# Attention and a mixture of experts on one Trainium2 core: the scale of w2 from sums of squares on ScalarE, the first block's scores in alternating row halves, the first block under the planner

## The chip, the cores and the metric

The kernel runs on one core of one Trainium2 chip, as one program. The metric is the device time of a run in microseconds (us). The engines are TensorE (PE for its matmuls, PEld for its weight loads), VectorE (DVE), ScalarE (ACT), GpSimd (POOL) and SyncE (SP), which here only issues DMAs. Each engine works through its own queue in order; semaphores tie the queues together.

## The reference

Attention comes first, over 4 batches of 8 heads, 768 positions and 64 columns. Each query sees the keys within 16 positions of it and one summary per block of 32 keys (the maximum of the keys, the mean of the values):

```python
k_sum = k.reshape(B, H, nb, block, D).max(axis=3)
v_sum = v.reshape(B, H, nb, block, D).mean(axis=3)
scores_l = scale * q @ k.T          # masked to |i - j| < 16
scores_s = scale * q @ k_sum.T + log(32)
a = softmax(concat(scores_l, scores_s)); out = a @ concat(v, v_sum)
```

Its output, as 3072 tokens of 512 columns, goes through four experts of 1024 hidden columns, and every token takes all four:

```python
p = domain_probs / (domain_probs.sum(-1) + 1e-9)
for e in range(4): out += p[:, e:e+1] * (maximum(x @ w1[e], 0) @ w2[e])
```

## The kernel before, in words

**Tiles.** Attention goes in 64 pieces: 96 queries of 4 heads each (`n` counts them, 16 to a batch). The experts take tokens in eight blocks of 384 (`tb`). Eight pieces make a block. The first block (pieces of queries 0 to 383 of batch 0) has code of its own, `first_tokens`, since no expert can start without it. Blocks 0 and 1 then go through the experts alone for experts 0 and 1 (stages `[0]` and `[1]` of `plan`, full-precision products `ph` and `po`); after that blocks go in pairs (`PAIRS`; pair 0 is blocks 0 and 1 with experts 2 and 3, pairs 1 to 3 have all four). A pair's first product is done in seven half-size products instead of eight (`pha`, `phb`, `phc`, `phd`), from sums and differences of tokens (`x_operands`, tiles `x_` and `x_t`) and weights (`w1_operands`, tiles `w1g`), each split in two 16-bit parts.

**A piece of the first block.** `scores` makes the products of 96 queries with 128 keys and 24 summaries, head by head, in two halves (two heads each, one PSUM tile `psc` each, from a pool of two); `maxima` on VectorE adds the mask and takes each row's maximum, `exps` on ScalarE the exponentials, `turn` transposes them on TensorE (`pT`), `gather` multiplies with the values (`pav`), `divide` normalises on VectorE, `x_turn` transposes again, `x_part` writes the two parts `xh` and `xl` of the tokens. A head's 64 columns lie in 64 of the 128 rows of the array: heads 0 and 2 of a piece in the upper half, 1 and 3 in the lower.

**Scales.** The 16-bit parts need a scale per expert. For each of w1 and w2 of an expert, `scan` loads the weights once more in eight tiles of 128x512 (`ws`, two buffers), and `largest` takes each row's largest magnitude on VectorE into `wmax`: 64 reductions for four experts. After an expert's last tile `scales_of_weights` takes the maximum (`wm`), and `scales` turns it by TensorE, spreads it and inverts it in a chain of small VectorE steps (`dg`, `big`, `scale`, `one`). Only then can that expert's `w1g` and `w2s` be made.

**What sets the order.** All instructions are recorded as steps and given out by a planner, `order_of`. It simulates the engines with costs per step (`Step.PE`, `Step.ACT` and so on, `SPARE` above them), takes at each moment the ready step that is due first, does this several times forward and backward (`ROUNDS`) and keeps its shortest plan. Steps before `in_order` keep the order in which they were written: in the kernel before, the whole first block does on every engine, with an order by hand (`KEYS`, `T0`, `STEPS`), and on SP besides. In which order attention's steps are recorded among the experts' is set by `ENDS`: the piece that attention has reached at the end of each stage. `XFREE` gives odd pieces below that number a second set of buffers, and `early` says how long before a stage's end the next pair's `x_operands` are recorded. Nearly every instruction is issued by one helper line, L373 in the profile of the kernel before.

## Time and profile before

| | us |
|---|---|
| median of 3 runs | 1080.83 (1080.18 to 1082.72) |
| the profiled execution, its own time | 1079.39 |
| its span, first to last instruction | 1077.5 |
| TensorE busy | 1051.8 (98%) |
| VectorE, ScalarE, GpSimd busy | 866.0, 730.2, 607.2 |
| mean granted TensorE clock | 0.995 |

The profiled execution is 1.89 us longer than its span, and 1.44 us under the median. In rows of a timeline the first column is the start in us from the span's start, the second the duration; a bracket at the end is idle time of that engine just before, and what ended it. In rows by stretch, each engine has its busy time in that stretch and its number of instructions, then come the granted clock, the busy share of the DMA engines and GB/s. In rows of groups, the two numbers behind the bar are busy us and mean ns of one. In rows by tile, the three durations are the least, the median and the largest in ns, and the two numbers after them the first and the last start.

### The profile page before, as it was taken

The page shows a single profiled execution, that of the slowest core. Times are in us where ns is not written, and L with a number is a line of the kernel's source. Part 1 is how long each engine was busy: PE and PEld are TensorE (multiplying, and loading weights), DVE is VectorE, ACT ScalarE, POOL GpSimd, SP SyncE. Part 2 cuts the span into 40 slices and gives each one's busy share as a digit, 9 for nine tenths or more (in the row PEclk, how much of TensorE's full clock was granted, in tenths as well). Part 3 has the DMA queues.
Part 4 walks back from the last instruction along what each step waited for, and adds up shares of the span by engine and source line. Part 5 has one row for each costly group of instructions (what it writes and reads, how often), then busy time and mean ns, then how long its engine had stood idle before and what let it go on. Part 6 is the DMA issues. An engine that isn't in the chain of part 4 may idle for free.

```text
span 1077.5 us, 22082 instructions
## 1 busy us (share of the span) xinstructions
PE 1051.8 (98%) x7497; PEld 707.7 (66%) x7497; DVE 866.0 (80%) x2102; ACT 730.2 (68%) x1992; POOL 607.2 (56%) x716
## 2 busy tenths in 40 slices
PE   9988999899999999999999999999999999999998
PEld 7977888654554555555555568686775567686867
DVE  6898889988877867988988897998767775969473
ACT  5776688887864744976977796988545763748170
POOL 2599588877743211852856887896532352717050
PEclk9999999989999999999999999999999999999999
DMA  8789887987888889789676664657422440424001
GB/s 287 212 202 244 227 220 198 274 270 198 240 245 253 253 232 254 220 268 263 207 231 170 167 176 126 176 163 217 116 83 89 135 149 16 162 66 151 1 15 59
DMA packets 172897, 194.95 MB, mean 181 GB/s; under 512 B 80368, under 2 KB 117232, under 8 KB 172784
## 3 DMA queue, kind: packets, MB, share of 16 engines
q1 hardware_dynamic: 172784, 193.55, 62.3%
q8 instruction: 58, 0.95, 0.4%
q14 instruction: 55, 0.45, 0.1%
HBM read 141.33 MB, written 35.65 MB: 164 GB/s over the span
## 4 chain that ended last, share of the span: by engine, by line
PE 66%; DVE 5%; POOL 2%; ACT 2%; DMA 1%; issue 1%; SPq 0%; DVEq 0%; POOLq 0%; ACTq 0%
PE po L373 16%; PE phb L373 13%; PE pha L373 8%; PE pob L373 7%; PE poa L373 5%; PE phd L373 4%; PE phc L373 4%; PE poc L373 3%; PE pod L373 2%; PE psc L373 2%; PE px L373 1%; POOL w2g L373 1%; DVE wr L373 1%; DMA wr<-in_w2L 1%; ACT ms L373 0%
## 5 line engine op out<-in xcount | busy, mean ns | idle before, releaser
L373 PEld LDWEIGHTS <-w1g 128*128 128x128 f16 x2352 | 229.2, 98 | 174.2 <-issue 13.0
L373 PEld LDWEIGHTS <-h 128*128 128x128 f16 x1764 | 171.0, 98 | 115.9 <-issue 0.5
L373 PE MATMUL po<-w2s,h 128*128 128x512 f16 x1008 | 239.6, 379 | 0.0
L373 PE MATMUL phb<-x_t,w1g 128*128 128x384 f16 x1008 | 195.3, 327 | 4.6 <-DVE phc L373 1.9
L373 POOL TENSOR_TENSOR w2g<-wr,w2g 128x512 f16<-128x512 f32 (+1 forms) x80 | 90.1, 1133 | 114.3 <-ACT w2g L373 112.1
L373 PE MATMUL pha<-x,w1g 128*128 128x384 f16 x672 | 133.3, 329 | 2.9 <-DVE nb L373 2.9
L373 ACT ACTIVATE ms<-ms,nb 96x152 f32<-96x152 f32 x256 | 104.0, 414 | 15.5 <-DVE nb L373 15.2
L373 PEld LDWEIGHTS <-hs 128*128 128x128 f16 x1008 | 98.0, 98 | 12.7 <-issue 0.4
L373 POOL TENSOR_TENSOR v<-qv,v 128x256 f16<-128x256 f32 (+1 forms) x56 | 45.7, 816 | 104.6 <-ACT v L373 89.7
L373 DVE CUSTOM_DVE_ANT_0 ms<-psc,c_sb 96x152 f32<-96x152 f32 x256 | 69.1, 305 | 31.3 <-PE psc L373 30.5
L373 POOL TENSOR_TENSOR h<-r,h 128x384 f16<-128x384 f32 x56 | 57.1, 1025 | 54.1 <-ACT h L373 51.5
L373 ACT CAST w2g<-wr 128x512 f16<-128x512 f32 (+1 forms) x112 | 61.6, 562 | 32.2 <-DVE wr L373 18.7
L373 POOL TENSOR_TENSOR w<-wr,w 128x512 fp32r<-128x512 f32 x48 | 65.3, 1368 | 26.2 <-ACT w L373 20.3
L373 DVE TENSOR_TENSOR aw<-ms,aw 96x512 f16<-96x512 f32 (+1 forms) x104 | 69.7, 686 | 6.3 <-ACT aw L373 6.3
L373 PE MATMUL ph<-xh,w 128*128 128x384 f32 x256 | 69.4, 343 | 5.1 <-ACT w L373 3.6
L373 PE MATMUL phd<-x_t,w1g 128*128 128x384 f16 x336 | 65.6, 326 | 2.6 <-POOL w1g L373 1.7
L373 PE MATMUL phc<-x,w1g 128*128 128x384 f16 x336 | 66.1, 326 | 0.0
L373 PE MATMUL poa<-w2g,h 128*128 128x256 f16 x504 | 65.4, 273 | 0.4 <-DVE nb L373 0.4
L373 PE MATMUL pob<-w2g,hs 128*128 128x256 f16 x504 | 64.0, 273 | 0.3 <-DVE poc L373 0.3
L373 POOL TENSOR_TENSOR ks<-kr,ks 128x304 fp32r<-128x304 f32 x56 | 53.3, 952 | 16.3 <-ACT ks L373 15.7
L373 PE MATMUL po<-w,hh 128*128 128x512 f32 x192 | 60.8, 396 | 0.0
L373 ACT ACTIVATE wr<-wr,scalew 128x512 f32<-128x512 f32 x72 | 51.8, 719 | 11.2 <-DMA wr<-in_w2L 7.7
(195 smaller groups left out, 2350.1 us busy)
## 6 DMA issues: line engine op xcount, KB each, us to landing
wr<-in_w2L SPq DMA_DIRECT2D x112, 256.0 KB, 3.3
w1g<-wdg SPq DMA_DIRECT2D x34, 512.0 KB, 4.1
w1g<-wdg SPq DMA_DIRECT2D x34, 384.0 KB, 3.8
ws<-in_w1L SPq DMA_DIRECT2D x32, 256.0 KB, 3.8
ws<-in_w2L SPq DMA_DIRECT2D x32, 256.0 KB, 3.8
wx<-in_w1L SPq DMA_DIRECT2D x32, 256.0 KB, 4.7
wdg<-w1g SPq DMA_DIRECT2D x16, 512.0 KB, 4.5
wd<-w2s SPq DMA_DIRECT2D x16, 512.0 KB, 5.1
```

The costliest lines, as they stand in the source:

```text
L373: program.append(Step(self.key, lambda: getattr(self.engine, name)(*a, **kw), name, a, kw))
```

## The change

**Scales.** `largest` does w2 no longer on VectorE: ScalarE squares each tile (a little enlarged) and sums a row's squares by the way. `scales_of_weights` then takes the root of the largest sum by a logarithm and an exponential on ScalarE, and a factor `W2_TOP` goes into the scale and out of the mixing weights. w1 stays as it was.

**Scores of the first block.** Both halves of a piece are one step group now, glued (nothing may come between), and its products alternate between the upper and the lower half of the array.

**Order.** The first block is given out by the planner on TensorE, ScalarE, VectorE and GpSimd; on SP it keeps its written order. The planner knows smaller costs for products in half the rows, a cost for the change between array shapes (`SWITCH`), the cost of the long accumulating activation, 5% instead of 10% to spare, and it does 24 rounds instead of 10.

**Pace.** At the end of stage `[1]` attention's steps have been recorded up to piece 24.5 instead of 26.5, at the end of pair 0 up to 35 instead of 36.5; later stages end where they did. `XFREE` goes from 28 to 24, and pair 0's `x_operands` are recorded from the start of stage `[1]`.

```diff
-ENDS = (17.52,26.5,36.5,53.0,72.0,74.0)
+ENDS = (17.52,24.5,35,53.0,72.0,74.0)
...
-XFREE = 28
+XFREE = 24
...
-SPARE, SPARE_DMA, LANES = 0.1, 300.0, 8
-ROUNDS = 10
+SPARE, SPARE_DMA, LANES = 0.05, 300.0, 8
+SWITCH = 80
+ROUNDS = 24
...
+                if k == "PE" and s.array != array:
+                    array = s.array
+                    t += SWITCH
...
     def largest(e, fc, which, raw):
-        V.tensor_reduce(
-            wmax[:, e, which, fc : fc + 1], raw, axis=AX.X, op=ALU.max, apply_absolute_value=True
-        )
+        to = wmax[:, e, which, fc : fc + 1]
+        if which:
+            A.activation(raw, raw, AF.Square, scale=ROUND, accum_out=to)
+        else:
+            V.tensor_reduce(to, raw, axis=AX.X, op=ALU.max, apply_absolute_value=True)
...
         V.tensor_reduce(m, wmax[:, e], axis=AX.X, op=ALU.max)
+        V.tensor_scalar_max(m[:, 1:2], m[:, 1:2], 2.0**-120)
+        A.activation(m[:, 1:2], m[:, 1:2], AF.Ln)
+        A.activation(m[:, 1:2], m[:, 1:2], AF.Exp, scale=0.5)
         s, back = scales(f"w{e}", m, 2)
...
+        V.tensor_scalar_mul(one[:, 2:3], s[:, 1:2], W2_TOP)
...
-            def scores(half):
-                t["psc", half] = ps_sc.tile([P, 2, 256], F32, name=f"psc{n}_{half}", tag="sc")
-                for j in (half, half + 2):
-                    o = t["psc", half][:QB, j // 2, :]
-                    r = slice((j % 2) * D, (j % 2 + 1) * D)
-                    PE.matmul(
-                        o[:, 0:KW], qr[r, j // 2, :], kch[2 * g + j // 2][r, w0 : w0 + KW], start=True, stop=True
-                    )
-                    PE.matmul(o[:, KW:KA], qr[r, j // 2, :], ksr[r, 2 * g + j // 2, :], start=True, stop=True)
+            def scores():
+                begin = len(program)
+                room, tag = (ps_mm, "mm") if m in () else (ps_sc, "sc")
+                for half in range(2):
+                    t["psc", half] = room.tile([P, 2, 256], F32, name=f"psc{n}_{half}", tag=tag)
+                for j in range(0, G, 2):
+                    for own in (True, False):
+                        for half in range(2):
+                            r = slice(half * D, (half + 1) * D)
+                            hp = 2 * g + j // 2
+                            o = t["psc", half][:QB, j // 2, 0:KW] if own else t["psc", half][:QB, j // 2, KW:KA]
+                            keys = kch[hp][r, w0 : w0 + KW] if own else ksr[r, hp, :]
+                            PE.matmul(o, qr[r, j // 2, :], keys, start=True, stop=True)
+                for s in program[begin + 1 :]:
+                    s.glued = True
...
-    in_order.update(dict.fromkeys(("PE", "ACT", "DVE", "POOL"), len(program)))
+    in_order.update(dict.fromkeys(("PE", "ACT", "DVE", "POOL"), 0))
...
-                early = first_us if nxt == 3 else first_us + second_us if nxt == 0 else 0.0
+                early = first_us if nxt == 3 else 2 * first_us + second_us if nxt == 0 else 0.0
```

**Where instructions stand now.** The first place is TensorE at the start of the first block, from the first piece's scores on (`psc_0` and `psc_1` are its two halves, `k_78` and `k_79` the keys of two pairs of heads, `ksr` the summaries, `pvf` the means of the values). Before:

```order
L373 MATMUL psc_0_117<-k_78,qv_0_82 96x128
L373 MATMUL psc_0_117<-ksr_92,qv_0_82 96x24
L373 MATMUL psc_0_117<-k_79,qv_0_82 96x128
L373 MATMUL psc_0_117<-ksr_92,qv_0_82 96x24
L373 MATMUL psc_1_120<-k_78,qv_0_82 96x128
L373 MATMUL psc_1_120<-ksr_92,qv_0_82 96x24
L373 MATMUL psc_1_120<-k_79,qv_0_82 96x128
L373 MATMUL psc_1_120<-ksr_92,qv_0_82 96x24
L373 MATMUL pvf_121<-vn_101,c_sb 120x256 x2
```

And now:

```order
L383 MATMUL psc_0_117<-k_78,qv_0_82 96x128
L383 MATMUL psc_1_118<-k_78,qv_0_82 96x128
L383 MATMUL psc_0_117<-ksr_92,qv_0_82 96x24
L383 MATMUL psc_1_118<-ksr_92,qv_0_82 96x24
L383 MATMUL psc_0_117<-k_79,qv_0_82 96x128
L383 MATMUL psc_1_118<-k_79,qv_0_82 96x128
L383 MATMUL psc_0_117<-ksr_92,qv_0_82 96x24
L383 MATMUL psc_1_118<-ksr_92,qv_0_82 96x24
L383 MATMUL pT_127<-c_sb,ms_119 128x96
L383 MATMUL pvf_121<-vn_101,c_sb 120x256 x2
```

Each product of one half now stands next to the same product of the other; and one transpose of the piece's exponentials has come ahead of the value means. Further on in the same block four of the expert's first products (`ph_0_0` to `ph_0_3`) and the scores of pieces 8 and 9 now stand among the last pieces, where they came behind them.

In the same block, the queue of SP between the last loads of queries and the loads of piece 8 (`kr_113`, `qv_114`; `ws` are tiles to scan, `wr` weights to split). Before:

```order
L373 DMA ws_1_445<-in_w1L 128x512
L373 DMA ws_1_458<-in_w2L 128x512
L373 DMA wr_2_110<-in_w2L 128x512
L373 DMA ws_2_460<-in_w1L 128x512
L373 DMA ws_2_465<-in_w2L 128x512
L373 DMA ws_3_488<-in_w1L 128x512
L373 DMA wr_3_111<-in_w2L 128x512
L373 DMA kr_113<-in_kT 128x2x128
L373 DMA qv_114<-in_qvL 64x288 x2
```

And now:

```order
L383 DMA ws_0_425<-in_w2L 128x512
L383 DMA pw<-in_dpL 128x96
L383 DMA ws_0_412<-in_w1L 128x512
L383 DMA wr_2_110<-in_w2L 128x512
L383 DMA wr_3_111<-in_w2L 128x512
L383 DMA kr_113<-in_kT 128x2x128
L383 DMA qv_114<-in_qvL 64x288 x2
```

Two scanned tiles stand ahead of piece 8's loads now, where seven did.

The second place is VectorE at the start of pair 0: in each kernel the eight rows that end with the first maximum of the scores whose PSUM tiles the pair's first products take over (`psc_0_762` before, `psc_0_735` now). Before:

```order
L373 TENSOR_TENSOR xr_3_598<-xr_3_598 128x192
L373 TENSOR_TENSOR ms_743<-ms_743,rs_745 96x608
L373 TENSOR_REDUCE wmax<-ws_5_766 128x1
L373 TENSOR_REDUCE wmax<-ws_5_768 128x1
L373 TENSOR_TENSOR x_t_580<-xr_2_596,x_t_580 128x2x96
L373 TENSOR_TENSOR x_t_580<-xr_3_598,x_t_580 128x2x96
L373 SCALAR_TENSOR_TENSOR acc_623<-po_0_1_724,pw,acc_623 128x512
L373 ISA ms_759,nb_760<-psc_0_762,c_sb 96x152
```

And now:

```order
L383 TENSOR_TENSOR x_t_517<-xr_3_540,x_t_517 128x2x96
L383 TENSOR_TENSOR aw_257<-ms_715,aw_257 96x512
L383 SCALAR_TENSOR_TENSOR acc_608<-po_0_0_700,pw,acc_608 128x512
L383 TENSOR_TENSOR aw_257<-ms_715,aw_257 96x4x24
L383 TENSOR_TENSOR w1g_1_744<-wx_3_711,w1g_1_744 128x256
L383 SCALAR_TENSOR_TENSOR acc_609<-po_0_1_701,pw,acc_609 128x512
L383 TENSOR_REDUCE wmax<-ws_5_739 128x1
L383 ISA ms_732,nb_733<-psc_0_735,c_sb 96x152
```

One scan stands there instead of two, the pair's last `x_t` parts are done earlier, and six parts of `w1g` stand ahead of `acc_609`, where five stood ahead of `acc_623`. On TensorE the value products of a piece (`px`) stood right behind the pair's first six products; the next ones come 78 products later now.

The third place is ScalarE in pair 0's first expert, where the scale of expert 3 is made (`wm_796` is the pair of maxima). Before, ScalarE had one `ACT_TABLE_LOAD`, at its very start. Now there are nine; two of them here:

```order
L383 CAST w1g_3_804<-wx_6_747 128x256
L383 COPY phb_2_3_835<-pha_2_3_834 128x384
L383 ACT_TABLE_LOAD
L383 ACTIVATE wm_796<-wm_796 128x1
L383 CAST w1g_3_804<-wx_7_748 128x256
L383 ACT_TABLE_LOAD
L383 ACTIVATE wm_796<-wm_796 128x1
L383 CAST w1g_3_805<-wx_7_748 128x256
L383 ACTIVATE h_2_4_817<-pha_2_2_810 128x384
```

Before, the same stretch had the copies and casts alone. The other three experts' scales have the same five rows in the middle, each with one other instruction between the two loads, or two.

24 lines of the change are left out of this document (15 added, 9 removed).

## The prediction, as written before the changed kernel was run

> **What bounds the kernel now.** I read the page's shares first, then busy time by stretch, then the waits inside the stretches that have any.
>
> ```profile
> PE 1051.8 (98%) x7497; PEld 707.7 (66%) x7497; DVE 866.0 (80%) x2102; ACT 730.2 (68%) x1992; POOL 607.2 (56%) x716
> ```
>
> TensorE is busy 98% of the 1077.5 us. So there are two ways to gain: give TensorE less to do, or close the 25.7 us in which it idles. The rows by stretch say where these lie (PE is the first number with a bracket, then PEld, DVE, ACT, POOL; the granted clock follows).
>
> ```profile
> 0.00:20.00 20.00, 18.23 (x124) 13.27 (x124) 11.28 (x47) 9.39 (x24) 5.58 (x21) 1.00 0.93 335
> 20.00:40.00 20.00, 19.75 (x173) 17.37 (x171) 17.20 (x74) 14.45 (x42) 3.46 (x7) 1.00 0.52 158
> 40.00:60.00 20.00, 18.30 (x126) 16.48 (x125) 18.95 (x48) 15.97 (x48) 18.24 (x18) 1.00 0.75 224
> 60.00:80.00 20.00, 18.88 (x127) 14.72 (x125) 17.82 (x48) 15.20 (x51) 19.55 (x19) 1.00 0.89 216
> 80.00:100.00 20.00, 17.47 (x143) 14.50 (x141) 19.10 (x46) 13.80 (x43) 19.68 (x22) 1.00 0.97 239
> 100.00:207.00 107.00, 105.98 (x708) 90.77 (x709) 93.34 (x256) 81.61 (x244) 82.95 (x99) 1.00 0.86 232
> 207.00:217.00 10.00, 3.78 (x33) 2.31 (x32) 10.00 (x19) 9.19 (x28) 9.84 (x12) 0.75 0.81 227
> 217.00:230.00 13.00, 12.79 (x64) 7.08 (x64) 12.05 (x24) 9.81 (x29) 8.98 (x12) 0.80 0.92 265
> 230.00:260.00 30.00, 27.58 (x173) 15.00 (x171) 26.06 (x65) 25.24 (x66) 22.92 (x29) 1.00 0.70 200
> 300.00:310.00 10.00, 8.58 (x63) 4.63 (x61) 7.37 (x28) 7.40 (x22) 4.82 (x6) 1.00 0.98 331
> 310.00:1077.50 767.50, 760.45 (x5498) 489.47 (x5495) 597.85 (x1361) 495.16 (x1308) 382.01 (x438) 1.00 0.54 158
> ```
>
> Behind 310 us only 7 of 767.5 us are idle: nothing is to be had there, only to be lost. The idle time lies in 40 to 101 us, where GpSimd is full (57.5 of 60), and at the start of pair 0, 207 to 217, where VectorE, ScalarE and GpSimd are all full and TensorE works 3.78 of 10 us. In the first block (7 to 40 us) TensorE itself is the limit: 19.75 of 20, VectorE 17.2, GpSimd only 3.46.
>
> **The first block's scores.** Here is one half of a piece by itself, and a place where a second half and the next piece's first half happened to run together.
>
> ```profile
> 12.87 0.53 PE L373 MATMUL psc<-k,qv 64*96 64x128 f32 x4
> 13.15 0.36 PE L373 MATMUL psc<-ksr,qv 64*96 64x24 f32 x4
> 13.35 0.43 PE L373 MATMUL psc<-k,qv 64*96 64x128 f32 x2
> ...
> 15.51 0.46 PE L373 MATMUL psc<-k,qv 64*96 64x128 f32 x2
> 15.80 0.27 PE L373 MATMUL psc<-ksr,qv 64*96 64x24 f32 x2
> 15.92 0.43 PE L373 MATMUL psc<-k,qv 64*96 64x128 f32 x2
> 16.19 0.27 PE L373 MATMUL psc<-ksr,qv 64*96 64x24 f32 x2
> 16.39 0.38 PE L373 MATMUL pav<-c_sb,xt 96*128 96x96 f32 x2
> ```
>
> Alone, a half (two heads) takes 15.51 to 16.39, 0.88 us; a piece 1.76. At 12.87 four passes appear in one row: two heads, one of each array half, done in 13.35 - 12.87 = 0.48 us. That is what the changed order does everywhere, so a piece costs 2 x 0.48 = 0.96, 0.80 less. Eight pieces give 6.4, less the 0.40 that this one place had already saved: 6.0 us. VectorE is next. In 20 to 40 us it has 2.8 us to spare, so over the block's 33 us about 4.6; scans leave the block (the order shows five fewer tiles loaded ahead of piece 8) and about as much other VectorE work comes in ahead of the last pieces. The scores of a piece now also need both PSUM tiles free, so they wait for all four maxima of the piece before. I take **-4.5**, between 0 (VectorE takes over at once) and -6.
>
> **40 to 101 us.** These are TensorE's waits there:
>
> ```profile
> 55.67 0.44 PE L373 MATMUL ph<-xh,w 128*128 128x384 f32 x1 [1.56 <-ACT w L373]
> 70.64 0.40 PE L373 MATMUL px<-awT,v 128*64 128x192 f16 x6 [1.12 <-DMA awT<-aw]
> 91.44 0.62 PE L373 MATMUL ph<-xh,w 128*128 128x384 f32 x2 [0.73 <-POOL w L373]
> 97.30 0.61 PE L373 MATMUL ph<-xh,w 128*128 128x384 f32 x2 [0.64 <-POOL w L373]
> 100.87 0.45 PE L373 MATMUL ph<-xh,w 128*128 128x384 f32 x1 [1.55 <-ACT w L373]
> ```
>
> 5.6 us, all for weight splits and pieces that ScalarE and GpSimd deliver late. GpSimd has no idle time left here but 16.5 us in 20 to 40. Why it could not start earlier stands on SP:
>
> ```profile
> 35.59 0.33 SPq L373 DMA_DIRECT2D wr<-in_w2L  x1
> 35.97 0.43 SPq L373 DMA_DIRECT2D kr<-in_kT  x1
> ```
>
> Piece 8's keys are asked for at 35.97, behind weight tiles that wait for buffers which the hand-written order frees late. In the new order the weight splits of the first block come as soon as they can, and two scans instead of seven stand before that load. So GpSimd gets some of its work earlier, and VectorE loses half its scans. But the first block also ends earlier, which asks for the same weights sooner. I take **-3**, between 0 and -5.6.
>
> **The start of pair 0.** TensorE's three waits, and VectorE's rows before the last of them:
>
> ```profile
> 209.63 0.82 PE L373 MATMUL phd<-x_t,w1g 128*128 128x384 f16 x4 [1.70 <-POOL w1g L373]
> 213.21 0.45 PE L373 MATMUL px<-awT,v 128*64 128x192 f16 x4 [2.76 <-DMA awT<-aw]
> 217.21 3.68 PE L373 MATMUL pha<-x,w1g 128*128 128x384 f16 x11 [1.98 <-DVE nb L373]
> ```
>
> ```profile
> 213.60 1.26 DVE L373 TENSOR_REDUCE wmax<-ws 128x1 f32<-128x512 f32 x2
> 214.78 1.24 DVE L373 TENSOR_TENSOR x_t<-xr,x_t 128x192 f16<-128x192 f32 x2
> 216.61 0.30 DVE L373 CUSTOM_DVE_ANT_0 ms<-psc,c_sb 96x152 f32<-96x152 f32 x1
> ```
>
> The maxima that free `pha`'s PSUM tile stand behind two scans and two `x_t` parts. And why is it all crammed there? The scale of expert 2:
>
> ```profile
> L373 DVE TENSOR_REDUCE wm<-wmax x4: 156/159/160, 149.4 to 493.0; 128x2 f32<-128x16 f32 x4
> L373 DVE TENSOR_SCALAR one<-scalew x4: 141/143/147, 200.8 to 503.6; 128x1 f32<-128x1 f32 x4
> ```
>
> The maxima are there at 149.4, the scale only at 200.8, and no `w1g` can be made before it; two fewer pieces of attention ahead of this point leave all three engines room. Of a piece alone, VectorE has four maxima and three long products. The order now has one scan instead of two ahead of the maxima, the last `x_t` parts earlier, and no `px` among the first products (which takes away the wait of 2.76 for a transposing DMA that stood in TensorE's queue). The price of the place: 6.2 idle in 207 to 217; then the clock, 0.80 over 13 us, 2.6 lost; and 0.25 of 3.78, 0.9. Together 9.7, with 2.4 more in 230 to 260. I take **-7**, between -2 (only the `px` wait goes) and -12.
>
> **ScalarE's new work.** The rows: a table load (the only one before), the nearest long activation, the read of an accumulator, and the reduction that it replaces.
>
> ```profile
> 0.73 1.28 ACT L373 ACT_TABLE_LOAD   x1 [0.73 <-PEq L1716]
> ...
> L373 DVE TENSOR_REDUCE wmax<-ws 128x1 f32<-128x512 f32 x64 | 42.6, 673 | 0.6 <-DMA ws<-in_w2L 0.6
> ...
> L373 ACT CAST w<-wr 128x512 fp32r<-128x512 f32 x52 | 31.7, 615 | 2.0 <-DMA wr<-in_w1L 0.9 <-PE po L373 0.7 <-DMA wr<-in_w2L 0.3
> ...
> L373 ACT ACTIVATION_READ_ACCUMULATOR ms<-ms,nb 96x1 f32 x224 | 42.4, 189 | 0.0
> ```
>
> VectorE loses 32 x 0.67 = 21.5 us. ScalarE gets 32 x (0.615 + 0.19) = 25.7 us, and eight table loads with eight one-column activations: for each expert 2 x 1.28 + 2 x 0.2 (estimated from the accumulator's read, one column too) + about 0.4 for a cast of half the row's columns between them = 3.4 us in which its queue moves nothing that TensorE waits for. Spread over 500 us the squares fit into its idle 32%; the four stops come in one piece. Queued behind the one shown by the order are `h_2_4` and the next PSUM evictions of pair 0, with TensorE behind them. A stop costs TensorE nothing while the seven open products keep it fed, at most its 3.4 us: 0 to 13.6 in all. Expert 3's scale is also needed within pair 0, so its chain gets longer by the same 3.4. I take **+2**, half a microsecond a stop: of the idle 25.7 the rows above put only 3.1 on ScalarE. [...]
>
> **Later attention.** 1.5 pieces move from pair 0 into pair 1, and VectorE, ScalarE and GpSimd have 22%, 35% and 50% to spare behind 310 us. **+1**, for the odd wait, between 0 and +3. The 1.4 idle at 300 to 310 I leave. `SPARE`, `SWITCH` and `ROUNDS` act only through the order: no cost of their own.
>
> **Sum**: -4.5 - 3 - 7 + 2 + 1 = -11.5. The profiled execution took 1079.39, 1.44 under the median of its runs; from it the sum gives 1067.9. For the median of the changed kernel I say **1068.5**, a part of that distance up.
>
> **Rivals.**
>
> *The gain stays hidden* (chance 0.17): the first block is held by VectorE at once (17.2 of 20 already, and two-tile scores wait for more of it), GpSimd stays full to 101 us, and only the `px` wait goes; or the halves do not run together in this order. Then -2 - 2 + 2 + 1, about **1078 to 1080**; with a little from the first block 1076. For it: full VectorE rows everywhere up to 260. Against: those engines lose work there, and the row at 12.87 shows the overlap.
>
> *ScalarE's stops decide* (0.11; slower). In 207 to 230 ScalarE is at 19 of 23 us, the scan's squares of expert 3 come into the same stretch, and the stop for expert 3 falls behind it. If each of the four stops reaches TensorE whole and the clock falls behind it as it did behind 207 to 217 (2.6 lost), that is 4 x 6.0 = 24, against 14.5 gained, 1 us of backlog added: **about 1090**. It is slower than before from 3.4 us a stop on. Against it: the planner can put PSUM evictions ahead of the loads, and two of the stops fall in stretches in which TensorE was never waiting. [...]
>
> *Everything goes* (0.14): -6 - 5.6 - 12 + 1: **1057**.
>
> *As summed* (0.58): **1061 to 1076**, centre 1068.5.
>
> About 0.2%, 2.2 us, is what a measurement of this kernel tells from no change. Faster: 0.58 + 0.14 + 0.07 of the hidden gain = 0.79. Same: 0.10. Slower: 0.11. The range, 1056 to 1079, leaves out the slower case and the hidden gain's upper half, and the tail of the best case.
>
> **What would show it.** Right: a piece's scores in rows of x4 with about 0.96 us each; TensorE's first `ph` before 33 us; GpSimd's idle in 20 to 40 well under 16; 207 to 217 (or its counterpart near 200) with TensorE over 8 of 10 and no clock under 0.9; nine table loads of 1.28 with little idle time of TensorE behind them; behind 310 us idle time still under 9. Wrong: waits of TensorE on ScalarE of 2 us and more right behind table loads; a first block as long as before with VectorE full; new waits on `nb` between 310 and 560, from the attention moved there.

## The result, and the profile after

The changed kernel took 1094.57 us (median of 6 runs, 1087.91 to 1098.55), the kernel before 1080.48 us beside it: a ratio of 1.0123, 95% interval 1.0102 to 1.0144. That is slower by about 13 us, where 12 us less was forecast. The profiled execution took 1097.22 us, its span 1095.3. The six times follow the mean granted clock of their runs: 1087.91 and 1089.78 us at 0.995 and 0.994, 1094.43 to 1098.55 us at 0.983 to 0.986. In this and all that follows, ratios leave out the slow runs, those over 1.5% above the fastest of their kernel (one of `e4_rows`, two each of `e10_plan` and `e16_halves`), and medians take in all.

Busy time of the engines, from the page of the changed kernel:

```profile
PE 1060.2 (97%) x7497; PEld 712.2 (65%) x7497; DVE 853.5 (78%) x2078; ACT 756.4 (69%) x2072; POOL 610.1 (56%) x716
```

TensorE has the same 7497 products, and yet 8.4 us more busy time (1051.8 before): some run at a lower clock. Its idle time went from 25.7 to 35.1 us. The rows by stretch of the changed kernel, in the same cut as before, with the last 768 us in two:

```profile
0.00:20.00 20.00, 16.39 (x114) 10.86 (x116) 9.18 (x42) 7.24 (x18) 2.50 (x19) 0.91 0.90 321
20.00:40.00 20.00, 18.87 (x129) 15.73 (x126) 13.04 (x55) 12.95 (x39) 8.79 (x11) 0.57 0.41 123
40.00:60.00 20.00, 17.73 (x116) 15.23 (x117) 14.90 (x53) 14.01 (x44) 15.30 (x15) 0.84 0.56 160
60.00:80.00 20.00, 20.00 (x138) 17.61 (x136) 17.37 (x37) 15.40 (x44) 17.82 (x21) 0.99 1.00 237
80.00:100.00 20.00, 20.00 (x148) 17.08 (x147) 17.43 (x47) 14.43 (x48) 17.52 (x19) 1.00 0.89 235
217.00:230.00 13.00, 13.00 (x98) 7.97 (x97) 10.65 (x23) 12.28 (x35) 10.88 (x14) 1.00 0.80 246
230.00:260.00 30.00, 25.62 (x152) 13.97 (x151) 25.52 (x70) 27.76 (x76) 19.83 (x26) 0.94 0.82 235
310.00:560.00 250.00, 246.59 (x1615) 133.21 (x1614) 188.58 (x519) 183.24 (x526) 115.31 (x158) 1.00 0.84 249
560.00:1058.00 498.00, 486.75 (x3630) 329.76 (x3629) 391.26 (x818) 322.66 (x817) 266.98 (x283) 1.00 0.42 125
```

And the last two stretches of the kernel before:

```profile
310.00:560.00 250.00, 249.74 (x1635) 135.18 (x1633) 202.09 (x526) 166.37 (x483) 110.72 (x153) 1.00 0.82 242
560.00:1058.00 498.00, 494.71 (x3720) 340.19 (x3718) 390.16 (x824) 327.69 (x824) 271.29 (x286) 1.00 0.42 120
```

Three losses stand out. In the first block the granted clock is 0.57 in 20 to 40 us, where it was 1.00. In 230 to 260 TensorE idles 4.4 of 30 us (2.4 before), and 3.4 in 310 to 560 (0.3 before). And behind 560 us it idles 11.3 of 498 us where it idled 3.3; the row there has 90 products fewer. Two of the places where time was to be won did win it. 60 to 100 us has no idle time left (3.65 before). And the stall at the start of pair 0 is gone: the pair starts at 215.7 us now, and in the 12 us from there TensorE is busy for 11.9 at a clock of 1.00, where in the 12 us from 207.4 it was busy for 5.6 at 0.69.

Starts of single products tell where it adds up. The first `ph` starts at 37.6 us (37.7 before), but it does not mark the end of the first block any more: 24 `ph` now stand ahead of that block's last product, where 12 did. The 25th `ph` has the whole block ahead of it in both kernels, and in the changed one two more pieces' scores; it starts at 55.5 us instead of 43.5. Pair 0's first `phd` starts at 215.7 (207.4); its 48th and last at 308.4 (311.5), so that pair 0 has won back the loss; the 96th, half way through pair 1, at 438.0 (434.6), the 144th, the last of pair 1, at 568.9 (564.1), and the 336th at 1057.8 (1039.5). From the 144th to the 336th `phd`, nearly all of pairs 2 and 3, it is 488.9 us instead of 475.4. This last length is called "pairs 2 and 3" below.

### The profile page after: what moved, and what is told of

It reads as the page before. It is cut to its first block, busy times and chain, and to the rows that moved or that the text cites. A ratio compares the mean times of both kernels' runs of the same rounds, so it can differ in the third digit from the quotient of the medians.

```text
span 1095.3 us, 22142 instructions
## 1 busy us (share of the span) xinstructions
PE 1060.2 (97%) x7497; PEld 712.2 (65%) x7497; DVE 853.5 (78%) x2078; ACT 756.4 (69%) x2072; POOL 610.1 (56%) x716
## 4 chain that ended last, share of the span: by engine, by line
PE 55%; DVE 11%; ACT 3%; issue 2%; POOL 1%; DMA 1%; SPq 0%; DVEq 0%; ACTq 0%; POOLq 0%
PE po L383 15%; PE phb L383 10%; PE pob L383 7%; PE pha L383 6%; PE poa L383 4%; PE phd L383 3%; PE phc L383 3%; PE poc L383 2%; DVE wr L383 2%; PE pod L383 2%; PE psc L383 2%; DVE aw L383 1%; DVE s L383 1%; PE px L383 1%; DVE hs L383 1%
## 5 line engine op out<-in xcount | busy, mean ns | idle before, releaser
L383 PE MATMUL pha<-x,w1g 128*128 128x384 f16 x672 | 130.8, 326 | 0.4 <-DVE nb L383 0.2
L383 ACT ACTIVATE ms<-ms,nb 96x152 f32<-96x152 f32 x256 | 104.0, 414 | 22.5 <-DVE nb L383 21.3
L383 DVE TENSOR_TENSOR aw<-ms,aw 96x512 f16<-96x512 f32 (+1 forms) x104 | 80.9, 799 | 16.0 <-ACT aw L383 15.1
L383 ACT CAST w2g<-wr 128x512 f16<-128x512 f32 (+1 forms) x112 | 60.8, 563 | 37.0 <-DVE wr L383 22.4
L383 POOL TENSOR_TENSOR w<-wr,w 128x512 fp32r<-128x512 f32 x48 | 67.6, 1414 | 25.1 <-ACT w L383 22.6
L383 POOL TENSOR_TENSOR ks<-kr,ks 128x304 fp32r<-128x304 f32 x56 | 56.1, 1002 | 25.8 <-ACT ks L383 20.5
L383 POOL TENSOR_TENSOR qs<-qv,qs 128x192 fp32r<-128x192 f32 x56 | 36.8, 658 | 44.4 <-ACT qs L383 44.1
```

Of the source, the lines that this page charges most:

```text
L383: program.append(Step(self.key, lambda: getattr(self.engine, name)(*a, **kw), name, a, kw))
```

## Where it is lost: the three places in the trace

**The clock of the first block.** TensorE's waits of the changed kernel in the first 24 us, from its timeline:

```profile
8.71 0.30 PE L383 MATMUL pT<-c_sb,ms 96*128 96x96 f32 x1 [1.76 <-ACT ms L383]
15.34 0.65 PE L383 MATMUL pav<-vsf,sT 96*96 96x260 f32 x2 [0.66 <-ACT ms L383]
22.63 0.98 PE L383 MATMUL pav<-vsf,sT 96*96 96x260 f32 x2 [0.86 <-DVE sT L383]
```

and what the clock does behind the last of them:

```profile
16.00:20.00 4.00, 4.00 (x52) 3.57 (x53) 3.44 (x17) 2.54 (x8) 0.58 (x3) 1.00 0.89 324
22.00:24.00 2.00, 1.37 (x7) 1.12 (x7) 1.68 (x6) 1.81 (x6) 1.37 (x5) 0.72 0.61 152
24.00:32.00 8.00, 7.87 (x54) 6.58 (x53) 4.69 (x24) 5.13 (x15) 1.84 (x2) 0.50 0.29 99
32.00:40.00 8.00, 8.00 (x56) 6.96 (x55) 5.43 (x18) 4.17 (x13) 3.66 (x4) 0.50 0.58 168
40.00:44.00 4.00, 4.00 (x21) 3.50 (x21) 1.52 (x10) 1.80 (x5) 0.00 (x0) 0.58 0.69 186
```

From about 23 to 43 us TensorE is busy without a gap worth naming and runs at half its clock. That costs about 10 us of full-speed work in the place where TensorE sets the pace, most of the 12.0 us by which the 25th `ph` is late.

**The stops of ScalarE.** The table loads of expert 2's scale, ScalarE's timeline of the changed kernel:

```profile
156.01 1.28 ACT L383 ACT_TABLE_LOAD   x1
157.30 0.20 ACT L383 ACTIVATE wm<-wm 128x1 f32<-128x1 f32 x1
157.41 0.60 ACT L383 CAST w<-wr 128x512 fp32r<-128x512 f32 x1
158.03 1.28 ACT L383 ACT_TABLE_LOAD   x1
159.32 0.20 ACT L383 ACTIVATE wm<-wm 128x1 f32<-128x1 f32 x1
```

and two of TensorE's waits on the scales (each `wm` is turned by TensorE itself, into `pmw`):

```profile
169.02 0.38 PE L383 MATMUL pmw<-dgw,ones 2*128 2x2 f32 x2 [2.58 <-DVE dgw L383]
...
239.60 0.27 PE L383 MATMUL pmw<-c_sb,wm 128*2 128x128 f32 x1 [2.52 <-ACT wm L383]
```

The stop is 3.5 us long, about as forecast (3.4). But it reaches TensorE by a way that the forecast did not have, besides the one that it had. A late eviction, as the forecast had it, is behind one wait (2.38 us ahead of a `phb` at 475.31, for ScalarE, some 4 us behind a load). At the two products above it is TensorE's own little products of the scale that wait: they stand in its queue at the place that the planner chose, and the planner's cost of an activation has no table load in it. Behind the first of these waits the clock falls too, as the forecast's second rival had it:

```profile
168.00:172.00 4.00, 2.98 (x9) 2.42 (x10) 3.78 (x8) 4.00 (x13) 4.00 (x6) 0.71 0.53 151
```

**Pairs 2 and 3.** Here are the products that wait most in 560 to 1060 us (count, busy time, mean, idle time ahead and what ended it): before, after, and two runs that are told of below, `e14_noload` and `e9_keep`, which differ in `SPARE` alone (0.05 and 0.1). `SPARE` is the share that the planner adds to the durations of ScalarE, VectorE and GpSimd, not of TensorE.

```profile
L373 PE MATMUL phb<-x_t,w1g 128*128 128x384 f16 x598 | 115.4, 326 | 2.4 <-DVE phc L373 1.4 <-DVE phd L373 0.6 <-ACT phb L373 0.3
```

```profile
L383 PE MATMUL phb<-x_t,w1g 128*128 128x384 f16 x591 | 114.5, 326 | 7.3 <-DVE phc L383 3.4 <-DVE phd L383 2.0 <-ACT phb L383 1.6
L383 PE MATMUL pob<-w2g,hs 128*128 128x256 f16 x432 | 55.2, 273 | 2.4 <-DVE poc L383 2.4
```

```profile
L383 PE MATMUL phb<-x_t,w1g 128*128 128x384 f16 x588 | 113.9, 326 | 8.5 <-DVE phc L383 5.7 <-ACT phb L383 1.5 <-DVE phd L383 1.2
```

```profile
L383 PE MATMUL phb<-x_t,w1g 128*128 128x384 f16 x582 | 113.2, 326 | 4.1 <-DVE phc L383 3.2 <-DVE phd L383 0.6 <-ACT phb L383 0.2
```

With the smaller margin TensorE idles longer ahead of a `phb` for VectorE and ScalarE: 7.3 and 8.5 us in all, against 4.1 with the larger margin and 2.4 before.

## The experiments

Ratios are to the kernel before, run beside each kernel on the same chip, with their 95% intervals; 1‰ is 1.08 us. Every edit is made on the changed kernel unless the text says otherwise.

### One part undone at a time

**e1_spare.** The planner's margin as before.

```diff
-SPARE, SPARE_DMA, LANES = 0.05, 300.0, 8
+SPARE, SPARE_DMA, LANES = 0.1, 300.0, 8
```

> The changed kernel with the planner's margin back at 10% (SPARE 0.1); all else as changed. Its order is planned anew. Theory 1 (the planner's smaller margin made the later stages' order too tight): from expert products of pair 1's end on, the changed kernel lost about 11 us on the kernel before (from +7 at 560 us to +18 at the end); with the old margin this shrinks to under 4, and the time falls from 1094.6 to about 1084. Rival (the later loss comes from the work moved to ScalarE or from attention moved later): the later loss stays within 3 us of what it is, time 1091 to 1098.

Measured: 1084.29 us, 1.0027 (1.0008 to 1.0046); pairs 2 and 3 in 483.9 us. So the margin seems worth about 10 us, half of it in pairs 2 and 3. Not all of that need be the margin's: in 20 to 44 us the clock costs 6.8 us in this trace and 10.2 in the changed kernel's, by its rows of 4 us.

**e2_noload.** The logarithm becomes a square, which brings no table load of its own (with the same edit e14 has one load, e13 nine).

```diff
-        A.activation(m[:, 1:2], m[:, 1:2], AF.Ln)
+        A.activation(m[:, 1:2], m[:, 1:2], AF.Square)
```

> The changed kernel with the logarithm of the scale's root replaced by a square, which needs no other table: all instructions stand in the very same order on every engine, only the eight added table loads are gone (the scale is no longer the root of the largest sum, but is still divided out again). Theory 2 (the loads stop TensorE): the idle times of TensorE of 2.58, 2.52 and 2.38 us right behind loads at 169, 240 and 475 us shrink under 0.5 each, and the time falls by 6 to 9 us, to about 1087. Rival (the loads only fill time in which TensorE would have waited for VectorE anyway): it falls by under 2 us.

Measured: 1084.22 us, 1.0030 (0.9999 to 1.0060), ten runs between 1076.92 and 1090.69. One table load. The order of the instructions is that of the changed kernel, so waits can be set against each other. Of the changed kernel's waits of TensorE between 150 and 560 us these are gone or smaller: 2.58 to 0.54 us at `pmw`, and 2.52 (`pmw`), 1.75 (a `phb` at 299.94) and 2.38 us (a `phb` at 475.31) to nothing. Together that is 8.7 us. The medians differ by 10, the runs at like clocks by 8 to 9: the five at 0.997 or 0.998 here have a median of 1080.06 us against the changed kernel's 1087.91 and 1089.78, the other five 1088.03 against its 1094.43 to 1098.55.

This run shows something else. Its first block has the same products in the same order, with the same wait of 0.86 us (the one at 8.7 us is 1.29 us here, 1.76 in the changed kernel):

```profile
21.02 0.68 PE L383 MATMUL pav<-vsf,sT 96*96 96x260 f32 x2 [0.86 <-DVE sT L383]
```

and behind it the clock stays up:

```profile
22.00:24.00 2.00, 1.94 (x28) 1.62 (x26) 1.90 (x8) 1.05 (x3) 0.00 (x0) 1.00 0.94 271
24.00:32.00 8.00, 7.34 (x81) 6.08 (x80) 7.12 (x38) 7.96 (x25) 4.41 (x5) 1.00 0.39 116
32.00:40.00 8.00, 7.81 (x67) 6.70 (x67) 5.38 (x24) 6.45 (x20) 6.34 (x7) 1.00 0.75 201
```

Its first `ph` starts at 30.5 us instead of 37.6, its 25th at 46.1 instead of 55.5. Even at full clock that is not ahead of the kernel before (43.5): from 5 us on to this product TensorE waits for 6.2 us in all, 0.7 before, so the time saved in the scores has turned into waits. Five of its runs stand at a mean clock of 0.997 or 0.998 and 1076.92 to 1081.29 us, the other five at 0.984 to 0.989 and 1087.16 to 1090.69: one kernel, two times, 8 to 9 us apart.

**e3_hand.** The first block in its written order again.

```diff
-    in_order.update(dict.fromkeys(("PE", "ACT", "DVE", "POOL"), 0))
+    in_order.update(dict.fromkeys(("PE", "ACT", "DVE", "POOL"), len(program)))
```

> The changed kernel with the first block back in its hand-written order on all engines (scores still in alternating halves). Theory 3 (TensorE's waits in the planned first block make its clock fall to half for some 20 us): the clock in 0 to 60 us is 1.00 throughout, the first expert product comes before 35 us, and the time falls by 6 to 10, to about 1086; the runs scatter no more than 3 us. Rival (the planned order of the first block is not worse in itself, the loss lies behind it): 1092 to 1097.

Measured: 1098.65 us, 1.0168 (1.0134 to 1.0202), first `ph` at 42.8 us with the clock at 1.00 from 20 to 60. That is neither of the two expectations: the clock holds there, and the time is longer still. From 5 us to the 25th `ph` TensorE waits for 7.5 us (0.7 in the kernel before), 3.6 of them ahead of products that wait for VectorE's `xt`. The new scores fit the written order badly, and planning the block helps.

**e4_rows.** The kernel before with the row scores alone (the changed kernel's `scores`, one step in place of two, written order).

```diff
...
-                (v_ones,), (scores, 0), (scores, 1), (maxima, 0), ...
+                (v_ones,), (scores,), (maxima, 0), ...
```

> The kernel before with the scores of the first block in alternating halves alone (hand-written order kept, one key of the steps' table left out). By the rows a piece saves 0.80 us. Theory 4 (TensorE bounds the first block): 5 to 6 us less, 1075. Rival (VectorE takes over at once, or two-tile scores wait for all four maxima): within 1.5 us of 1080.5; the worst case is the clock again, if the freed time shows up as idle time of TensorE: slower than before.

Measured: 1090.99 us, 1.0070 (1.0039 to 1.0101), first `ph` at 45.2 us, pairs 2 and 3 in 474.8 us as before. Its rows by stretch:

```profile
30.00:40.00 10.00, 7.53 (x61) 6.24 (x59) 6.82 (x31) 5.17 (x15) 2.85 (x7) 0.79 0.53 160
40.00:50.00 10.00, 9.72 (x56) 8.53 (x56) 6.56 (x22) 5.23 (x15) 1.66 (x2) 0.70 0.75 213
```

No engine is full in 30 to 40 and TensorE works 7.53 of 10 us: it waits twice for VectorE's `xt`, 0.80 and 1.67 us, and behind the second wait the clock falls. From 5 us to the 25th `ph` its waits come to 7.0 us (0.7 before), 4.2 of them for `xt` and 1.4 at the scores. The loss in time goes with the clock: two of its runs are at 0.995 and take 1081.05 and 1081.56 us, as the kernel before. The saving in the products is real, 0.89 us a piece in the changed kernel's timeline (13.24 to the next product at 14.13; 1.76 before, taken in the same way):

```profile
13.24 0.46 PE L383 MATMUL psc<-k,qv 64*96 64x128 f32 x4
13.53 0.27 PE L383 MATMUL psc<-ksr,qv 64*96 64x24 f32 x4
13.65 0.44 PE L383 MATMUL psc<-k,qv 64*96 64x128 f32 x4
13.92 0.27 PE L383 MATMUL psc<-ksr,qv 64*96 64x24 f32 x4
14.13 0.47 PE L383 MATMUL pT<-c_sb,ms 96*128 96x96 f32 x3
```

but in this order it turns into waits, and into a loss where the clock falls behind them.

### The pacing, the planner alone, the maxima, two repairs together

**e5_pace.** The pacing of before.

```diff
-ENDS = (17.52,24.5,35,53.0,72.0,74.0)
+ENDS = (17.52,26.5,36.5,53.0,72.0,74.0)
-XFREE = 24
+XFREE = 28
-                early = ... 2 * first_us + second_us if nxt == 0 ...
+                early = ... first_us + second_us if nxt == 0 ...
```

> The change with its pacing undone: ENDS back to 26.5 and 36.5, XFREE back to 28, and pair 0 again fills attention for one first part and one second part, not two and one. Scores, squares, planned first block and the planner's constants stay. Theory P (the pacing loses the time, since it shifts the attention work of pair 0 and lets pairs 2 and 3 start late): near 1081, and pairs 2 and 3 (first product of pair 2 to the end of pair 3) back from 488.9 us to about 475. Theory Q (the time is lost at ScalarE's table loads and in the planner's smaller margins, the pacing is worth little either way): 1092 to 1098, pairs 2 and 3 still above 483 us.

Measured: 1093.87 us, 1.0094 (1.0061 to 1.0128), pairs 2 and 3 in 489.1 us: not the pacing. What the pacing does is seen all the same. Pair 0 takes 104.5 us again from its first to its 48th `phd` (92.7 in the changed kernel, 104.0 before), and the first half of pair 1 gives most of it back, 120.5 instead of 129.6 us.

**e6_plan.** The kernel before with the change's numbers of the planner.

```diff
-SPARE, SPARE_DMA, LANES = 0.1, 300.0, 8
-ROUNDS = 10
+SPARE, SPARE_DMA, LANES = 0.05, 300.0, 8
+ROUNDS = 24
-            return 420.0 * (1 + SPARE), 560.0 + 420.0 * SPARE
+            t = 420.0 if n < 200 else 175.0 + 0.85 * n
+            return t * (1 + SPARE), t * (1 + SPARE) + 140.0
```

> The kernel before with nothing but the planner's new constants: SPARE 0.05 instead of 0.1, 24 instead of 10 rounds, and the new cost of a ScalarE activation that sums. Its scores, maxima, first block in the written order and pacing are those of before. Theory Q (smaller margins and more rounds put dependent work closer together than the chip runs it, and this costs most of the time in pairs 2 and 3): 1087 to 1093, pairs 2 and 3 at 483 to 490 us instead of 475. Rival R (the planner's constants are harmless, and pairs 2 and 3 lose by the work that the change moves to ScalarE or by the pacing): 1078 to 1083, pairs 2 and 3 at 474 to 477 us.

Measured: 1088.48 us, 1.0081 (1.0036 to 1.0125), pairs 2 and 3 in 481.8 us instead of 475.4. The planner's numbers alone, with nothing of the kernel's work changed, cost 9 us.

**e7_max.** w2's scale from maxima on VectorE, so no squares and no root; the rest of the change stays.

```diff
-        if which:
-            A.activation(raw, raw, AF.Square, scale=ROUND, accum_out=to)
-        else:
-            V.tensor_reduce(to, raw, ...)
+        V.tensor_reduce(to, raw, ...)
...
-        A.activation(m[:, 1:2], m[:, 1:2], AF.Ln)
-        A.activation(m[:, 1:2], m[:, 1:2], AF.Exp, scale=0.5)
```

> The change with w2's scale again from maxima: VectorE takes the maximum of each piece as before, no squares, no Ln and no Exp on ScalarE, one table load in all. Row scores, planned first block, planner's constants and pacing stay. Theory Q (the squares and the stops of ScalarE cost about 10 us, the rest is the planner's): 1082 to 1087, no wait of 2.4 us of TensorE behind a weight's scale, pairs 2 and 3 still 483 us or more. Rival R (all of the loss is the work moved to ScalarE): 1076 to 1080 and pairs 2 and 3 at 475. Rival P (the squares unload VectorE and are worth their price; without them VectorE, 78% busy, gets later): 1095 or more.

Measured: 1092.40 us, 1.0105 (1.0074 to 1.0136): 1082.90 in the one run at a clock of 0.995, 1091.60 to 1094.81 in four at 0.983 to 0.989. Pairs 2 and 3: 485.8 us. The clock hides what was asked; `e17_max` asks it again.

**e8_both.** e1 and e2 together.

```diff
-SPARE, SPARE_DMA, LANES = 0.05, 300.0, 8
+SPARE, SPARE_DMA, LANES = 0.1, 300.0, 8
...
-        A.activation(m[:, 1:2], m[:, 1:2], AF.Ln)
+        A.activation(m[:, 1:2], m[:, 1:2], AF.Square)
```

> The change with both repairs that helped alone: the root's logarithm replaced by a squaring on the resident table (one table load instead of nine; the scale of w2 is another number, the work and the order of the instructions are the same) and SPARE back at 0.1. If the two gains (10 us each against the change) add up, as theory Q has it: 1073 to 1077, under the kernel before. If they are one and the same gain (both only take TensorE past the same waits at 160 to 240 us, theory R): 1082 to 1086.

Measured: 1076.09 us, 0.9941 (0.9921 to 0.9961), faster than before. The two gains add: 8.6‰ against e1, 8.9‰ against e2. And TensorE's order is that of e1, whose waits of 2.72 (`pmw`), 1.82 (`pha`) and 1.43 us (`pmw`) at 228, 268 and 473 us are gone. All six of its runs are at a clock of 0.987 to 0.992; the row of its first block says why, and what was left to win:

```profile
20.00:40.00 20.00, 18.29 (x120) 15.74 (x118) 11.83 (x49) 12.03 (x34) 6.47 (x9) 0.53 0.50 138
```

### Holding the clock

**e9_keep.** e8 with three idle products of the warm-up's zero tile ahead of each first-block piece's first product into `pav`.

```diff
                 t["pav"] = ps_av.tile([P, 512], F32, name=f"pav{n}", tag="av")
+                for _ in range(3):
+                    PE.matmul(t["pav"], z[:, 0:P], z, start=True, stop=True)
```

> The version with both repairs (squaring in place of the logarithm, SPARE 0.1; 1076.09 us) plus three idle products of a zero tile (128x512, the warm-up's) into each first-block piece's value tile before its first real product: 24 more products, about 5 us of TensorE at full clock, standing where TensorE waits for a piece's softmax. Nothing that is computed changes. Theory C (the first block is long because waits of 0.66 to 1.8 us let the granted clock fall to half, which then lasts about 20 us): the granted clock stays at 1.00 from 20 to 44 us (now 0.55 and 0.50 in 20 to 40), the first product of the weights starts at 29 to 33 us instead of 38.4, and the time falls by 4 to 8 us to 1068 to 1072, although work is added. Rival W (the waits themselves decide, the clock is only their shadow): no gain, 1076 to 1081.

Measured: 1069.40 us, 0.9897 (0.9881 to 0.9913), all six runs from 1068.98 to 1072.43 us at a clock of 0.994 to 0.998. Its first `ph` starts at 34.2 us (38.4 in e8), its 25th at 49.7 (52.5). Some of the idle products of its timeline, and the first block's stretch:

```profile
16.16 0.81 PE L383 MATMUL pav<-z 128*128 128x512 bf16 x3
21.10 0.47 PE L383 MATMUL pav<-z 128*128 128x512 bf16 x1 [1.23 <-DVE sT L383]
```

```profile
20.00:40.00 20.00, 17.38 (x155) 14.11 (x157) 15.36 (x65) 15.59 (x46) 9.58 (x13) 0.91 0.57 160
```

With added work the time is 4.4‰ less (4.8 us; 6.7 between the medians), and the mean clock of every run is above e8's. The clock did not stay at 1.00 all through 20 to 44 us, which was expected of it: in this trace it is 0.66 in 20 to 24 us and 0.92 in 24 to 28, and then back at 1.00, where e8's is 0.50 from 24 to 40.

The 4.8 us are not the price of the clock, though. The planner gave the instructions behind the first block another order too. In the two traces e9 is ahead by 4.7 us at pair 0's first `phd` (197.2 and 201.9 us), behind by 1.1 at the 144th (553.3 and 552.1), and wins 6.0 in pairs 2 and 3 (477.6 and 483.6), where the clock is full in both. What the clock is worth is seen where one order has two clocks, in e2: 8 to 9 us. That it is a cause and not a shadow rests on that and on the changed kernel's trace, where products that TensorE does without a gap take nearly twice their time (`ph` from `xh` 613 ns in the mean in 24 to 43 us, 334 in the median of all). What makes it fall in one run and not in another is open.

**e10_plan.** e8 with the rest of the planner's old numbers.

```diff
-SWITCH = 80
-ROUNDS = 24
+SWITCH = 0
+ROUNDS = 10
...
-            t = 420.0 if n < 200 else 175.0 + 0.85 * n
-            return t * (1 + SPARE), t * (1 + SPARE) + 140.0
+            return 420.0 * (1 + SPARE), 560.0 + 420.0 * SPARE
```

> The version with both repairs (1076.09 us) with the rest of the planner's numbers back too: 10 rounds instead of 24, no cost for a switch of the array's form, and the old cost of a ScalarE activation that sums. Theory Q (the new planner constants also hold the 8 us that pairs 2 and 3 still lose, 483.6 us against 475.4 in the kernel before): pairs 2 and 3 at 474 to 478 us, time 1067 to 1072. Rival S (pairs 2 and 3 lose by other means, such as what the squares and the later attention leave to do): 483 us again, 1074 to 1079.

Measured: 1077.19 us, 0.9977 (0.9948 to 1.0006), from 1069.42 at a clock of 0.997 to 1087.51 at 0.981; pairs 2 and 3 in 477.1 us. The clock hides the answer again; `e12_best` has it.

**e11_halves.** e8 with `scores`, `STEPS` and the products' planned cost of before, in the planned first block.

```diff
-            t = (65.0 + 1.75 * n) * (0.53 if w.ap[0][1] == D else 1.0)
+            t = (65.0 + 1.75 * n)
...
-            def scores():
+            def scores(half):
...
-                (v_ones,), (scores,), (maxima, 0), ...
+                (v_ones,), (scores, 0), (scores, 1), (maxima, 0), ...
```

> The version with both repairs (1076.09 us) with the scores of before: each half's four products into one tile, released apart, and their old cost in the planner; the first block stays planned. Theory G (the row scores are 0.9 us shorter a piece but start only when both tiles are free and give up their half-way release, so they bring TensorE no earlier end of the first block): first product of the weights within 2 us of 38.4, time within 2 us of 1076. My forecast's step (each of 8 pieces 0.8 us cheaper, worth about 4.5 us): 1079 to 1082.

Measured: 1087.18 us, 1.0059 (1.0037 to 1.0080), beyond both expectations. Its first block in rows:

```profile
20.00:40.00 20.00, 19.48 (x95) 15.89 (x95) 9.64 (x42) 9.37 (x26) 6.64 (x12) 0.50 0.23 60
40.00:60.00 20.00, 19.59 (x95) 15.99 (x94) 9.88 (x35) 10.34 (x29) 6.20 (x7) 0.50 0.52 140
```

40 us at half the clock with TensorE at 39 of 40, first `ph` at 55.6 us. In a planned first block the row scores are worth more than forecast: without them the clock is at 0.50 for 40 us, where e8's is low for some 20.

### The sizes at a held clock

Since e9's runs lie within 3.5 us, where the changed kernel's lie within 10.6, the parts were taken out again with the idle products in place.

**e13_keep.** The changed kernel as it is, with e9's idle products alone.

> The changed kernel as it is (table loads, SPARE 0.05), with nothing but the 24 idle products added in the first block. Theory C (of the 14 us that the change loses, about half is the clock of the first block): 1084 to 1089, with a scatter of a few us instead of 10, and clock 0.993 or more in all runs. Rival W: 1093 to 1099, scatter as before.

Measured: 1083.99 us, 1.0019 (1.0005 to 1.0034), ten runs at 0.994 or more: 11.2 us less than the changed kernel. Not all of it is the clock: the changed kernel's two runs at 0.994 and 0.995 are 4 to 6 us slower than this. The new plan also places the stops better: two of them reach TensorE, with 1.52 and 2.38 us, where the changed kernel had 8.7.

**e14_noload.** e13 with the squaring of e2.

> The kernel of the run beside it (the change with 24 idle products) with the logarithm replaced by a squaring, so one table load instead of nine and the same order on every engine. With the first block's clock held, the difference of the two runs is the price of the eight table loads and what waits behind them: theory Q says 7 to 11 us (1076 to 1080 if the other stands at 1087); my forecast's price, about 2 us for all of ScalarE's new work, would leave less than 3 us between them.

Measured: 1079.61 us, 0.9984 (0.9971 to 0.9996): 3.5‰, 3.8 us less than e13, give or take 2. Without loads the idle products bring nothing by themselves: the five runs of e2 in which the clock held have a median of 1080.06 us. The same products in the two timelines, e13:

```profile
162.55 0.38 PE L383 MATMUL pmw<-dgw,ones 2*128 2x2 f32 x2 [1.52 <-DVE dgw L383]
...
229.43 0.27 PE L383 MATMUL pmw<-c_sb,wm 128*2 128x128 f32 x1 [2.38 <-ACT wm L383]
```

and e14:

```profile
162.82 0.27 PE L383 MATMUL pmw<-c_sb,wm 128*2 128x128 f32 x1
...
229.08 0.27 PE L383 MATMUL pmw<-c_sb,wm 128*2 128x128 f32 x1
```

1.52 + 2.38 = 3.9 us of waits are gone, and what is behind stays as it was: from the 48th to the 336th `phd` it is 753.7 us in e13 and 753.1 in e14. So the price of the eight loads is about the sum of the waits they leave on TensorE: 3.9 us in this plan, 8.7 in the changed kernel's.

e9 is e14 with `SPARE` 0.1, and 8.7‰ (9.4 us) faster. The rows for pairs 2 and 3 of the two, e14:

```profile
560.00:1058.00 498.00, 486.06 (x3647) 332.45 (x3646) 389.13 (x803) 320.45 (x805) 266.44 (x280) 1.00 0.41 118
```

and e9:

```profile
560.00:1058.00 498.00, 493.03 (x3740) 342.09 (x3739) 391.69 (x810) 319.84 (x804) 267.33 (x280) 1.00 0.41 118
```

Between these two rows 7.0 us of idle time are gone. That makes four measurements of the margin: 9.6‰ (e1 against the change), 8.9‰ (e8 against e2), 8.7‰ (e9 against e14), and 8.1‰ with rounds and a cost besides (e6). The third is the cleanest, with idle products and nearly the same clock on both sides. Pairs 2 and 3 took 485.8 to 489.9 us in all seven versions of the change with 0.05, and 477.1 to 483.9 in all ten with 0.1. The kernel before took 475.4; where the 2 to 8 us that are left come from was not found.

**e12_best.** e9 with the planner's old numbers of e10.

> The version with both repairs, the idle products in the first block (1069.4 us) and the old planner constants throughout (10 rounds, no switch cost, old cost of a summing activation). If the 6.5 us that pairs 2 and 3 won by the old constants (477.1 us against 483.6) add to the 6.7 us of the idle products: 1061 to 1066. If the first block or pair 0 gives them back: 1067 to 1071.

Measured: 1073.90 us, 0.9925 (0.9905 to 0.9945). It lost 3 us; the 24 rounds and the new costs are no loss. e9 stayed the best.

**e15_pace.** e9 with e5's pacing of before.

> The version with both repairs and the idle products (1069.4 us) with the pacing undone: ENDS 26.5 and 36.5, XFREE 28, pair 0 fills one first part and one second part. With the first block's clock held the pacing is seen alone. My forecast's step (later attention costs about 1 us): 1067 to 1069. Rival P (the pacing is worth its place, since it gives pair 0 more work to stand beside its attention): 1071 to 1076.

Measured: 1078.76 us, 0.9981 (0.9963 to 1.0000). The profiled run is the slowest of the ten (1084.07 us). The stall at the start of pair 0 is back in it, in its rows by stretch and in the first of its waits in 195 to 310 us (sum, count, longest); the longest for `nb` comes at 282.8, late in the pair:

```profile
210.00:220.00 10.00, 6.13 (x37) 3.33 (x37) 8.01 (x23) 7.57 (x24) 9.84 (x11) 0.66 0.97 263
```

```profile
PE phd L383 <- POOL x_t L383: 4.5, 1, 4.5
PE pha L383 <- DVE nb L383: 3.7, 2, 3.5
```

Here the pacing is worth 8.4‰; with the margin at 0.05 and the clock free (e5) nothing of it was seen in the time. Its effect on the stall is shown, its worth in the changed kernel is not settled.

**e16_halves, e17_max, e18_hand.** e9 with the scores of before (as e11), with w2 from maxima (as e7), and with the written order in the first block (as e3); of each diff the line that says it:

```diff
+            def scores(half):
```

```diff
+        V.tensor_reduce(to, raw, axis=AX.X, op=ALU.max, apply_absolute_value=True)
```

```diff
+    in_order.update(dict.fromkeys(("PE", "ACT", "DVE", "POOL"), len(program)))
```

> The version with both repairs and the idle products (1069.4 us), with the scores of before: two halves in turn, each into its own tile, at their old cost in the planner. With the clock of the first block held, the difference is what the row scores are worth in a planned first block. My forecast's step (0.8 us a piece, 4.5 us in all): 1073 to 1075. If the 11 us between the two without idle products were the clock alone: 1068 to 1071.

> The version with both repairs and the idle products (1069.4 us), with w2's scale from maxima on VectorE again: no squares, no root, one table load. If moving the sums to ScalarE is worth something as long as no table switches come with it (VectorE gives up 21.5 us where it is nearly full): 1072 to 1077. If ScalarE's 25.7 us weigh as much as VectorE's: 1067 to 1071.

> The version with both repairs and the idle products (1069.4 us), with the first block in the written order on all engines instead of planned. If planning the first block is worth its place: 1075 to 1085, the first product of the weights at 38 us or later instead of 34. If the planned order only brought the clock's fall: 1066 to 1071.

Measured: e16 1079.13 us, 0.9972 (0.9947 to 0.9996), with clocks from 0.976 to 0.998, so that three idle products did not always hold it (its five runs at 0.995 or more have a median of 1077.08 us); e17 1072.45 us, 0.9922 (0.9907 to 0.9938); e18 1083.35 us, 1.0022 (1.0007 to 1.0037). By these the row scores are worth about 8 us (7 at a held clock), the squares about 2.7 and the planned first block 13.5, each when taken from e9 by itself. They do not add up (with pacing they make 33, and e9 is 11 us faster than before): the planner gives another order each time, and pairs 2 and 3 alone differ by up to 7 us between versions with the same margin, so 3 us more or less tell little.

## Why the forecast was wrong, step by step

**The sentence on the planner failed.** "`SPARE`, `SWITCH` and `ROUNDS` act only through the order: no cost of their own", said the forecast, and of the stretch behind 310 us, "nothing is to be had there, only to be lost". Both halves were at hand and were not put together. The order is indeed the only way in which the margin acts, and through it halving the margin loses 8.7 to 9.6‰, 9 to 10 us: about half of it in pairs 2 and 3 in two of the comparisons (e1, e8), nearly all in the cleanest (e9 against e14). In 310 to 1058 us, where under 9 us of idle time was a sign of being right, TensorE idles 14.7. Of `ROUNDS` and `SWITCH` the sentence held: undoing them won nothing (e12).

**The clock of the first block was no term of the sum.** The forecast priced a fall of the clock at the start of pair 0 and behind ScalarE's stops, but took the first block's 1.00 as given. The planned block with row scores has waits of 0.66 to 1.76 us, and behind them the clock halves for some 20 us in the trace; by their mean clocks, four of the six runs went that way. Worth: 8 to 9 us between runs of one kernel at the two clocks (e2), 5 to 11 between the changed kernel's own. So "TensorE's first `ph` before 33 us" came out wrong with 37.6, and right with 30.5 where the clock happened to stay (e2). The sign was a poor one: in the new order this product no longer stands behind most of the block.

**ScalarE's new work, +2, was mis-sized.** Nine table loads of 1283 ns came as said, and so did the stops (3.5 us where 3.4 was said). Of the four stops, half a microsecond each was expected to reach TensorE; the waits come to 8.7 us in the changed kernel (3.9 in e13). Against that may stand about 2.7 us for VectorE's relief (e17), no more than orders differ by among themselves. The forecast looked at the evictions queued behind the stop, and one of the four waits, 2.38 us, is of that kind. Two, 4.6 us together, are ahead of TensorE's own `pmw`, the turning of the scale, standing in order in its queue; how the fourth, 1.75 us and 60 us behind the nearest load, hangs on the loads was not followed. The sign "waits of TensorE on ScalarE of 2 us and more right behind table loads" was the one to watch. Next to a load no more time is lost: the cast ahead of it ends at 155.99, the load goes from 156.01 to 157.29, and the activation starts at 157.30. The price was in who waits.

**Scores, -4.5.** The size of a piece was right (0.89 us, 0.96 forecast), but the first block did not get shorter by it. At full clock (e2) the 25th `ph` starts 2.6 us later than in the kernel before, with 24 more products of scores ahead of it and 5.5 us more of waits: the time saved in products came back as waits, which the forecast allowed for with 1.5 of its 6.0 us. Against the old scores in the same planned block the new ones gain 7 to 8 us (e16), more than forecast; but with the old scores that block ends later than the written one did (25th `ph` at 60.8 us in e16, 52 without the 8.5 us that its clock lost, and 43.5 in the kernel before), so this is no gain on the kernel before. In the written order 3.6 of 7.5 us (e3) and 4.2 of 7.0 (e4) of the waits are for VectorE's `xt`. That both tiles must be free, the reservation that the forecast named, is behind at most the 1.4 us that e4 waits at the scores, and is not shown to decide.

**40 to 101 us, -3.** Right for 60 to 100, where 3.65 us of idle time are gone. 40 to 60 lost 0.6 more, at a clock of 0.84. (One of the five waits summed there, 1.12 us, was for a DMA and not for ScalarE or GpSimd.) Of this term and the scores' together little is left at full clock: e2's 97th `ph` starts at 82.2 us, 81.3 before, with 20 more products of other kinds ahead of it.

**Start of pair 0, -7, and later attention, +1.** The mechanism held: the stall is gone, pair 0 took 92.7 us from its first to its 48th `phd` instead of 104.0, the first half of pair 1 129.6 instead of 123.1. So 11.3 won and 6.5 given back, 4.8 in all, where -7 and +1 stood; part of both numbers is the attention that moved from one to the other. e15 shows the stall return with the old pacing. With the pacing alone undone (e5) the two stretches together are 2.6 us longer than in the changed kernel, and the time is not longer. The waits on `nb` feared for 310 to 560 did not come.

**The sum again.** The three losses that the runs show, about 9 for the margin, 8 to 9 for the clock where it falls and 8.7 for the stops, come to 26. The forecast with its +2 for ScalarE taken out is -13.5, which leaves +12 or 13; measured was 12.3‰, 13.3 us. That this comes out is partly luck: the -4.5 of the scores is not there at full clock, and the parts do not add up from one order to the next. So is it that e9, with the three undone, takes 1069.4 us, close to the 1068.5 of the forecast: its terms have other sizes. The rival "ScalarE's stops decide" (about 1090) came nearest in time. It was a part of the cause, waits and a fall of the clock behind one of them, next to two losses that it did not name.

**A version that beats both.** e9 is 1.03% faster than the kernel before. Its scale of w2 is not the root; e17, which takes the maxima as the kernel before does and leaves nothing out, is 0.78% faster.
